# Five moves in the order of DVE and ACT work, and four row transfers as one, in a fused attention and spectral-mix kernel

## The chip, the cores and the metric

One NeuronCore of a Trainium2 chip. The metric is the device time of one execution in microseconds (us), lower is better; where several runs are given, it is their median. The engines are named as the profile names them: PE (TensorE, matmuls), PEld (its weight loads), DVE (VectorE), ACT (ScalarE), POOL (GpSimd), SP (SyncE, which here only issues DMAs). SPq and ACTq are the queues from which DMAs are issued.

## The reference

q, k and v are 8 batches x 12 heads x 448 positions x 64, all float32.

```python
def _attn_ref(q, k, v, cap):
    scale = 1.0 / np.sqrt(q.shape[-1])
    scores = scale * np.matmul(q, k.transpose(0, 1, 3, 2))
    scores = cap * np.tanh(scores / cap)
    scores = scores - np.max(scores, axis=-1, keepdims=True)
    attn = np.exp(scores)
    attn = attn / (np.sum(attn, axis=-1, keepdims=True) + 1e-09)
    return np.matmul(attn, v)

def _moe_ref(x, w_theta, w_tok_r, w_tok_i, w_ch):
    theta = x @ w_theta
    zr, zi = x * np.cos(theta), x * np.sin(theta)
    y = np.einsum('ts,bsd->btd', w_tok_r, zr) + np.einsum('ts,bsd->btd', w_tok_i, zi)
    u = x + y
    return u + np.maximum(u @ w_ch, 0.0)
```

x is the attention's output as 8 x 448 x 768 (the 12 heads side by side).

## The kernel before

**Units.** The attention works on pairs of heads: 48 pairs, numbered k, six of them to a batch, and what a pair gives is one tile X[b, j] of 128 x 448. The mix works on a batch b of six such tiles (j from 0 to 5). A matmul of the mix is made from three products of a high and a low part (`split_x` makes them of X: the high part is a copy on ACT, the low part a subtraction on DVE), and a weight is brought into the same form in steps: a scaling, a `head` of four DVE instructions (L126 to L129), a copy (L131 or L133) and a `rest` of two subtractions (L137, L138).

**Slots.** The program is a row of slots. In slot s the scores of pair s are computed in two halves (on PE; L247, L258 or L268), each with a tanh (ACT, L287) and an exp (ACT, L299 or L293). Both halves use the same accumulator tile `s`, so the next half of scores can start only when the tanh has read the half before. In the same slot the products with v (`av`) and the row sums (`sums`, tile `r`) of pair k = s - 1 run on PE. Slots 0 to 7 are written out in `opening` (L603); from slot 8 on, six slots make a batch, and each takes a line of words from `part_scripts` (L558), one list for batch 0 (slots 8 to 13) and one for batches 1 to 6. What follows the last pair is in `TAIL`. Within the program every engine and every DMA queue runs its instructions in the order in which these words and calls stand (`manual_schedule`): an instruction that waits holds up all that is behind it on its engine.

**The words used below.** SA and SB: the two halves of scores, SB without its tanh, which is tB (with SAm, tA is the tanh of the first half). th, ch: the mix's two projections (`proj`, 18 matmuls a tile). high, low: the two parts of a rotated tile (ACT copy, then DVE subtraction). mix: the product with the token weights (21 matmuls). gain: the residual sum on DVE that reads mix's accumulator and adds it into X (L543). rotate: a DVE multiplication; turn: a transposition on DVE and a DMA to a DRAM buffer; back: four DMAs from it. prep: the split of a q/k pair into two parts on DVE (L216, L217). wa to we: the steps of the weights that stand in `WEIGHTS` for that slot. a, b, c: sums of the exps on DVE. norm: the multiplication of two X tiles by the inverse row sums (L453).

**Accumulators.** `th`, `ch`, `mx`, the sums `r` and the products of odd pairs come from one pool of three buffers (`psM`, L54). A new one takes the buffer of the one three before it, and its first matmul waits for the last reader of that buffer. For a mix, that is a `gain`; for a `ch` tile it is L551 (relu, sum with X, on DVE), which for the last tile of a batch stands behind the six `split_x` of the next batch (L547 to L552).

**Row sums of the first pairs.** For k below 8 a ones-matmul leaves the sums in four rows of an accumulator (0, 32, 64, 96). `invert` (L411) copies it to `rows` (DVE, L419) and four DMAs on SP (L421) reshape each row of 448 to 14 rows of 32 of a small tile. `spread` (L441) takes the reciprocal of that tile on DVE (L438), writes it to DRAM (L433) and reads it back four times as broadcasts (L449, tile `bc`). `norm` (L451) multiplies by `bc`.

**Slots 6 and 7 before** end so (L639 to L651): slot 6 splits X tiles 0 and 1, calls spread(5), then norm(2) and norm(3), then a weight step (a scaling on ACT), then splits tiles 2 and 3. Slot 7 calls norm(4), norm(5) and splits tiles 4 and 5.

Of the kernel before, what the change touches and what calls it, by code (L numbers as in the profile page):

```python
# [36 lines left out]
def softcap_attn_then_spectral_mix(ctx, tc, qk2, v, vj, cap, w_theta, w_tok, w_ch, sel, outT):  # L37
    nc = tc.nc
    B, NP, P, _, S = qk2.shape
# [4 lines left out]
    NJ = DM // P  # L44
# [3 lines left out]
    TB = S // 32  # L48
# [39 lines left out]
    def fill(n):  # L88

        t = psM.tile([P, 512], F32, tag="m", name=f"fill{len(fills)}")  # L90
        fills.append(t)
        for _ in range(n):
            nc.tensor.matmul(t[:32, :CP], ones_sb, ones_sb[:, :1].broadcast_to([CP, CP]), start=True, stop=True)
# [8 lines left out]
    class Split:  # L102
# [37 lines left out]
        def split(self):  # L140
            self.head()
            self.rest()
# [46 lines left out]
    def weights(s, pos):  # L189
        for word in WEIGHTS.get((s, pos), "").split():  # L190
            step = steps[word[-3:-1], int(word[-1])]
            {">": step.load, "*": step.scale, "#": step.vscale, "(": step.head, ")": step.rest}.get(word[0], step.split)()
# [30 lines left out]
    def load_v(k, queue=nc.scalar):  # L223
        if joint(k):
            n = NC3 + k % 2
            vt[k] = wk.tile([P, NC3 + 1, 2, D], F32, tag="v", name=f"v{k}", bufs=2)
            queue.dma_start(vt[k][:, :n], vj[k // NP, k % NP][:, :n])
        else:
            vt[k] = wk.tile([CP, 2, NCH, D], F32, tag="v", name=f"v{k}", bufs=2)
            queue.dma_start(vt[k], v[k // NP, k % NP])  # L230
# [45 lines left out]
    def qk_half(k, half):  # L276

        if not joint(k):
            if (k, half) != (0, 0):
                scores(k, half)  # L280
            rows = slice(0, CP)
        else:
            (quads if k < WHOLE else triples)(k, half)
            rows = slice(0, P)
        pp = pt[k, half] = wk.tile([P, 2, 2, S], F32, tag="xhl" if apart(k, half) else "p", name=f"p{k}_{half}", bufs=3)
        n = 1 if half and joint(k) and not ends(k) else 2
        return lambda: nc.scalar.activation(pp[rows, :n], sp[rows, :n, :, :S], AF.Tanh, scale=qscale[rows])  # L287
# [85 lines left out]
    def copy_x(k):  # L373
        if joint(k) and k % 2 == 0:
            return
        for n in (k - 1, k) if joint(k) else (k,):
            x = wk.tile([P, S], F32, tag="x", name=f"x{n}", bufs=12)
            nc.scalar.copy(x, ACC.pop(n)[:, :S])
            X[n // NP, n % NP] = x
# [3 lines left out]
    def direct(k):  # L383
        return k < DIRECT and not state["general"]
# [26 lines left out]
    def invert(k):  # L411

        if k % 2 == 0:
            return
        r = state.pop("r")
        ri = wk.tile([4 * TB, 32], F32, tag="rq", name=f"rq{k}", bufs=1)
        if direct(k):
            rows = wk.tile([P, S], F32, tag="ri", name=f"ri{k}", bufs=1)
            nc.vector.tensor_copy(rows, r[:, :S])  # L419
            for i in range(4):  # L420
                nc.sync.dma_start(ri[TB * i : TB * (i + 1), :], rows[32 * i : 32 * i + 1, :].rearrange("o (t i) -> o t i", i=32))  # L421
            summed[k] = ri
            return
        if state["general"]:
            nc.vector.tensor_scalar_add(ri, r[: 4 * TB, :32], 1e-9)
            nc.vector.reciprocal(ri, ri)
        else:
            nc.vector.reciprocal(ri, r[: 4 * TB, :32])
        keep(k, ri)

    def keep(k, ri):
        inverse[k] = dram.tile([2, 2, S], F32, tag="inverse", name=f"inverse{k}")
        nc.sync.dma_start(inverse[k].rearrange("n h (t i) -> (n h t) i", i=32), ri)  # L433

    def inverted(k):
        if k in summed:
            ri = summed.pop(k)
            nc.vector.reciprocal(ri, ri)  # L438
            keep(k, ri)

    def spread(k):  # L441
        inverted(k)
        if k not in inverse:
            return
        rows = inverse.pop(k)
        for n in (k - 1, k):
            bc[n] = wk.tile([P, S], F32, tag="bc", name=f"bc{n}", bufs=2)
            for hh in range(2):
                nc.sync.dma_start(bc[n][hh * D : (hh + 1) * D, :], rows[n % 2, hh : hh + 1, :].broadcast_to([D, S]))  # L449

    def norm(k):  # L451
        x = X[k // NP, k % NP]
        nc.vector.tensor_tensor(x, bc.pop(k), x, op=ALU.mult)  # L453
# [4 lines left out]
    def split_x(b, j, name):  # L458
        if j % 2 == 0:
            tag = "p" if name == "xs" and b == B - 1 else "xhl"  # L460
            state["xhl"] = wk.tile([P, 2, 2, S], F32R, tag=tag, name=f"{name}{b}_{j}", bufs=3)
        t = state["xhl"][:, j % 2]
        nc.scalar.copy(t[:, 0, :], X[b, j])
        nc.vector.tensor_tensor(t[:, 1, :], X[b, j], t[:, 0, :].bitcast(F32), op=ALU.subtract)
        XHL[b, j] = t
# [92 lines left out]
    def part_scripts(b):  # L558
        rows = [
# [9 lines left out]
        ]  # L569
        if b == 0:  # L570
            rows = [
# [9 lines left out]
            ]  # L581
        return [row.split() for row in rows]

# [19 lines left out]
    def opening(s):  # L603
        k = s - 1
        qk_half(s, 0)()
        if s == 0:
            fill(FILL["half"])
        weights(s, "a")
        exp_half(s, 0)
        if k >= 0:  # L610
            av(k)
            copy_x(k)
        load_v(s + 1, nc.sync)
        if k >= 0 and not split(k):
            sums(k, (0,))
        qk_half(s, 1)()
        if s == 0:
            fill(FILL["slot"])
        if k >= 0:
            if split(k):  # L620
                sums(k, (0,))
            elif split(k - 1):
                sums(k - 1, (1,))
            else:
                sums(k, (1,))
        load_qk(s + 2)
        weights(s, "b")
        for n in {4: (1,), 6: (3,)}.get(s, ()):
            spread(n)
        if s == 6:  # L630
            weights(s, "c")
        if k >= 0 and not split(k):
            invert(k - 1 if split(k - 1) else k)
            if not direct(k):
                spread(k)
        exp_half(s, 1)
        add_half(s, 0)
        add_half(s, 1)
        if s != 6:  # L639
            weights(s, "c")  # L640
        for n in {5: (0, 1), 7: (4, 5)}.get(s, ()):
            norm(n)
        if s == 6:
            for j in range(2):
                split_x(0, j, "xs")
            spread(5)
            norm(2)
            norm(3)
            weights(s, "d")
        for j in {6: range(2, 4), 7: range(4, NJ)}.get(s, ()):  # L650
            split_x(0, j, "xs")  # L651

    def slot(s):
        k = s - 1
# [138 lines left out]
```

## Time and profile before

| | |
|---|---|
| median of 3 runs | 904.56 us (902.23 to 904.97) |
| the profiled execution | 902.97 us, of which its span in the profile is 901.2 us |
| PE busy | 881.9 us, 98% |
| PEld busy | 656.0 us, 73% |
| DVE busy | 659.1 us, 73% |
| ACT busy | 595.0 us, 66% |
| mean granted TensorE clock | 0.998 |
| HBM, mean over the span | 124 GB/s |

A row of a timeline reads: start (us from the span's start), length in us, engine, line of the kernel, operation, out<-in, shape, count of merged instructions, and in square brackets how long the engine sat idle before it and whose end released it. Rows of one kind that follow each other are merged into one, as x8. Lengths of matmuls are modelled and overlap a little with the next.

### The profile page before, as it was taken

How to read it: one execution, taken by the hardware profiler on the slowest of the kernel's cores; microseconds unless marked ns; L12 is line 12 of the kernel's file. 1: busy time of each engine (PE TensorE's matmuls, PEld its weight loads, DVE VectorE, ACT ScalarE, POOL GpSimd, SP SyncE). 2: the span in 40 equal slices, each digit the busy share in tenths (PEclk: the TensorE clock that was granted, in tenths of full speed). 3: DMA queues.
4: the chain of work that ended last, by engine and by line, in shares of the span. 5: the costliest groups of instructions: out<-in, count | busy, mean ns of one | idle time of the engine just before them, and what ended most of it. 6: DMA issues, size and time to landing. Idle time of an engine off the chain costs nothing.

```text
span 901.2 us, 12590 instructions
## 1 busy us (share of the span) xinstructions
PE 881.9 (98%) x4848; PEld 656.0 (73%) x4848; DVE 659.1 (73%) x940; ACT 595.0 (66%) x599; POOL 1.1 (0%) x7
## 2 busy tenths in 40 slices
PE   8998999999999999999999999999999999999997
PEld 5332767678778777787777787877877877789996
DVE  6886898987975687757977569755897568765841
ACT  6986786578856687647974579546876669744320
POOL 0000000000000000000000000000000000000000
PEclk9999999999999999999999999999999999999999
DMA  7563176323633246132562126522262324501621
GB/s 269 192 199 101 57 260 222 110 88 99 203 91 107 90 132 194 44 122 64 164 193 74 61 72 196 152 85 93 94 205 79 113 84 143 162 19 36 213 64 64
DMA packets 68068, 112.88 MB, mean 125 GB/s; under 512 B 10400, under 2 KB 49824, under 8 KB 68000
## 3 DMA queue, kind: packets, MB, share of 16 engines
q1 hardware_dynamic: 62384, 103.01, 35.8%
q10 hardware_dynamic: 5616, 8.98, 3.3%
q8 instruction: 40, 0.66, 0.3%
q14 instruction: 28, 0.23, 0.1%
HBM read 78.73 MB, written 33.20 MB: 124 GB/s over the span
## 4 chain that ended last, share of the span: by engine, by line
PE 68%; DVE 17%; ACT 6%; DMA 4%; issue 3%; SPq 2%; DVEq 0%; POOL 0%; ACTq 0%; POOLq 0%
PE s L258 8%; PE a L359 6%; PE ch L472 6%; PE ch L474 6%; PE ch L473 6%; PE mx L537 6%; PE mx L538 5%; PE mx L539 5%; PE th L472 4%; PE th L473 4%; PE th L474 4%; DVE g_sb L500 4%; DVE g_sb L507 3%; ACT p L287 3%; PE s L247 3%
## 5 line engine op out<-in xcount | busy, mean ns | idle before, releaser
L287 ACT ACTIVATE p<-s,qscale 128x1792 f32<-128x1792 f32 (+1 forms) x96 | 166.4, 1734 | 119.1 <-PE s L258 106.4
L537 PE MATMUL mx<-wtk_h,zh 128*128 128x448 f32 x336 | 125.5, 374 | 4.2 <-DVE x L543 4.2
L539 PE MATMUL mx<-wtk_h,zl 128*128 128x448 f32 x336 | 123.0, 366 | 0.0
L538 PE MATMUL mx<-wtk_l,zh 128*128 128x448 f32 x336 | 122.8, 366 | 0.0
L472 PE MATMUL ch<-us,wch_h 128*128 128x448 f32 x288 | 107.0, 371 | 0.0
L472 PE MATMUL th<-xs,wth_h 128*128 128x448 f32 x288 | 106.7, 371 | 0.0
L474 PE MATMUL ch<-us,wch_l 128*128 128x448 f32 x288 | 105.7, 367 | 0.9 <-DVE wch_l L138 0.9
L473 PE MATMUL ch<-us,wch_h 128*128 128x448 f32 x288 | 105.7, 367 | 0.0
L474 PE MATMUL th<-xs,wth_l 128*128 128x448 f32 x288 | 105.3, 366 | 0.0
L473 PE MATMUL th<-xs,wth_h 128*128 128x448 f32 x288 | 105.3, 365 | 0.0
L299 ACT ACTIVATE p<-p,cap_sb 128x1792 f32<-128x1792 f32 (+1 forms) x56 | 99.9, 1784 | 0.5
L359 PE MATMUL a<-p,v 128*64 128x448 f32 x480 | 99.0, 548 | 0.0
L537 PEld LDWEIGHTS mx<-wtk_h,zh 128*128 128x128 f32 x336 | 63.1, 188 | 16.5 <-issue 10.7
L529 DVE TENSOR_TENSOR zl<-g_sb,zh 128x896 fp32r<-128x896 f32 x48 | 51.2, 1078 | 32.5 <-ACT zh L523 18.3
L551 DVE SCALAR_TENSOR_TENSOR x<-ch,x 128x448 f32<-128x448 f32 x48 | 29.8, 621 | 59.5 <-PE ch L474 59.5
L359 PEld LDWEIGHTS a<-p,v 128*64 128x64 f32 x480 | 30.9, 136 | 51.5 <-issue 40.9
L539 PEld LDWEIGHTS mx<-wtk_h,zl 128*128 128x128 f32 x336 | 63.1, 188 | 5.3
L538 PEld LDWEIGHTS mx<-wtk_l,zh 128*128 128x128 f32 x336 | 63.1, 188 | 4.9
L523 ACT CAST zh<-g_sb 128x896 fp32r<-128x896 f32 x48 | 44.7, 937 | 26.8 <-PE mx L538 15.9
L472 PEld LDWEIGHTS th<-xs,wth_h 128*128 128x128 f32 x288 | 54.1, 188 | 9.3 <-issue 4.4
L472 PEld LDWEIGHTS ch<-us,wch_h 128*128 128x128 f32 x288 | 54.0, 188 | 9.3 <-issue 3.1
L474 PEld LDWEIGHTS ch<-us,wch_l 128*128 128x128 f32 x288 | 54.1, 188 | 6.2 <-DVE wch_l L138 1.3
(97 smaller groups left out, 1478.7 us busy)
## 6 DMA issues: line engine op xcount, KB each, us to landing
turn<-g_sb SPq DMA_DIRECT2D x48, 448.0 KB
g_sb<-turn SPq DMA_DIRECT2D x192, 112.0 KB
qk_sb<-in_qk SPq DMA_DIRECT2D x39, 448.0 KB
bc<-inverse SPq DMA_DIRECT2D x96, 112.0 KB
out_dram<-x SPq DMA_DIRECT2D x48, 224.0 KB
v<-in_vj ACTq DMA_DIRECT2D x20, 256.0 KB
g_sb<-in_wth SPq DMA_DIRECT2D x6, 768.0 KB
qk<-in_qk SPq DMA_DIRECT2D x9, 448.0 KB
```

What stands on the lines that cost most here:

```text
L258: nc.tensor.matmul(sp[:, i, hh, :S], kk[k][rows, 1, at : at + P], qq[k][rows, 0, :], start=n == 0, stop=n == 2)
L287: return lambda: nc.scalar.activation(pp[rows, :n], sp[rows, :n, :, :S], AF.Tanh, scale=qscale[rows])
L299: nc.scalar.activation(pp[rows], pp[rows], AF.Exp, scale=cap_sb[rows])
L359: nc.tensor.matmul(acc[hh * D : (hh + 1) * D, :S], va[:, c, hh, :], pt[k, c // 2][:, c % 2, hh, :], start=c == 0, stop=False)
L472: nc.tensor.matmul(acc[:, :S], wh[:, j, ms], t[:, 0, :], start=j == 0, stop=False)
L473: nc.tensor.matmul(acc[:, :S], wh[:, j, ms], t[:, 1, :], start=False, stop=False)
L474: nc.tensor.matmul(acc[:, :S], wl[:, j, ms], t[:, 0, :], start=False, stop=j == NJ - 1)
L523: nc.scalar.copy(zh.rearrange("p c (g t) -> p c g t", g=4), turned(j))
L529: nc.vector.tensor_tensor(zl.rearrange("p c (g t) -> p c g t", g=4), turned(j), zh.bitcast(F32).rearrange("p c (g t) -> p c g t", g=4), op ...
L537: nc.tensor.matmul(acc[:, :S], zh[:, c, :], wtk_h[:, c, :], start=c == 0, stop=False)
L538: nc.tensor.matmul(acc[:, :S], zh[:, c, :], wtk_l[:, c, :], start=False, stop=False)
L539: nc.tensor.matmul(acc[:, :S], zl[:, c, :], wtk_h[:, c, :], start=False, stop=c == NC2 - 1)
```

## The change

Five edits of the order, and one of a transfer:

- `invert`: the four DMAs of one row each become one DMA, which reads every 32nd partition of `rows`.
- Slot 6 of `opening`: spread(5) moves behind norm(2) and norm(3). The splits of tiles 2 and 3 move from the end of slot 6 to slot 7, ahead of norm(4) and norm(5).
- Third slot of batches 1 to 6: gain0 moves from behind `turn4 back3` to right behind low2, ahead of rotate4.
- Third slot of batch 0 (slot 10): tA moves ahead of high1.
- Last slot of batch 0 (slot 13): norm moves from ahead of SB, and prep from ahead of `wb`, to behind `wc`.

```diff
-            for i in range(4):
-                nc.sync.dma_start(ri[TB * i : TB * (i + 1), :], rows[32 * i : 32 * i + 1, :].rearrange("o (t i) -> o t i", i=32))
+            nc.sync.dma_start(ri, rows[::32, :].rearrange("n (t i) -> n t i", i=32))
...
-            "SA high0 low0 high1 sincos1 low1 c- V x v SB mix0 high2 tB prep q rotate3 turn3 low2 rotate4 turn4 back3 gain0 r inv"
+            "SA high0 low0 high1 sincos1 low1 c- V x v SB mix0 high2 tB prep q rotate3 turn3 low2 gain0 rotate4 turn4 back3 r inv"
             " rotate5 turn5 back4 back5 bc A B mix1 gain1 mix2",
...
-                "wa SAm fold5 high0 a- low0 high1 tA sincos1 low1 b- V x v SB mix0 c- high2 tB q rotate3 turn3 low2 gain0"
+                "wa SAm fold5 high0 a- low0 tA high1 sincos1 low1 b- V x v SB mix0 c- high2 tB q rotate3 turn3 low2 gain0"
...
-                "SA V x v norm SB tB wa prep q wb A ch3 wc a B ch4 b c ch5",
+                "SA V x v SB tB wa wb A ch3 wc prep q norm a B ch4 b c ch5",
...
-        for n in {5: (0, 1), 7: (4, 5)}.get(s, ()):
-            norm(n)
+        if s == 5:
+            norm(0)
+            norm(1)
         if s == 6:
             for j in range(2):
                 split_x(0, j, "xs")
-            spread(5)
             norm(2)
             norm(3)
+            spread(5)
             weights(s, "d")
-        for j in {6: range(2, 4), 7: range(4, NJ)}.get(s, ()):
-            split_x(0, j, "xs")
+        if s == 7:
+            for j in range(2, NJ):
+                if j == 4:
+                    norm(4)
+                    norm(5)
+                split_x(0, j, "xs")
```

## Rows read from the trace of the kernel before

**Rows 1.** Page, busy us (share) xinstructions; PE's waits: total us, times, longest.

```profile
PE 881.9 (98%) x4848; PEld 656.0 (73%) x4848; DVE 659.1 (73%) x940; ACT 595.0 (66%) x599; POOL 1.1 (0%) x7
...
PE mx L537 <- DVE x L543: 4.2, 6, 0.7
```

**Rows 2.** Timeline of PE, slots 2 and 6 to 8.

```profile
21.94 1.76 PE L247 MATMUL s<-qk_sb 64*112 64x448 f32 x8 [1.85 <-ACT p L287]
...
70.82 1.70 PE L404 MATMUL r<-p,ones_sb 112*32 112x448 f32 x8
76.70 2.60 PE L247 MATMUL s<-qk 64*112 64x448 f32 x8 [4.18 <-ACT p L287]
...
81.66 1.74 PE L268 MATMUL s<-qk_sb 64*64 64x448 f32 x16
...
89.61 0.98 PE L268 MATMUL s<-qk_sb 64*64 64x448 f32 x8
```

**Rows 3.** Timeline of ACT in slots 6 to 8.

```profile
73.90 1.09 ACT L463 CAST xs<-x 128x448 fp32r<-128x448 f32 x2 [4.71 <-DVE x L453]
74.90 1.75 ACT L287 ACTIVATE p<-s,qscale 112x1792 f32<-112x1792 f32 x1
...
79.46 1.74 ACT L287 ACTIVATE p<-s,qscale 112x1792 f32<-112x1792 f32 x1
...
86.42 1.75 ACT L287 ACTIVATE p<-s,qscale 128x1792 f32<-128x1792 f32 x1
```

**Rows 4.** Timeline of DVE in slots 6 and 7.

```profile
68.23 1.16 DVE L464 TENSOR_TENSOR xs<-x,xs 128x448 fp32r<-128x448 f32 x2 [1.75 <-ACT xs L463]
73.04 0.34 DVE L438 RECIPROCAL rq<-rq 56x32 f32<-56x32 f32 x1 [3.65 <-DMA rq<-ri]
...
75.57 0.39 DVE L126 TENSOR_SCALAR swk_t<-swk_raw 128x448 int32<-128x448 int32 x1
...
84.76 1.15 DVE L453 TENSOR_TENSOR x<-bc,x 128x448 f32<-128x448 f32 x2
```

**Rows 5.** Timeline of SP's DMA queue in slot 6.

```profile
68.57 3.25 SPq L421 DMA_DIRECT2D rq<-ri  x4
```

**Rows 6.** Windows: us, busy PE, PEld, DVE, ACT, POOL, PEclk (granted clock), DMA share, GB/s.

```profile
77.50:80.90 3.40, 3.40 (x12) 0.87 (x10) 3.26 (x7) 3.40 (x3) 0.00 (x0) 0.50 0.79 256
```

**Rows 7.** Timelines of ACT and PE in slot 10.

```profile
121.79 0.94 ACT L523 CAST zh<-g_sb 128x896 fp32r<-128x896 f32 x1 [1.17 <-DMA g_sb<-turn]
...
124.44 0.98 PE L268 MATMUL s<-qk 64*64 64x448 f32 x8 [0.86 <-ACT p L287]
```

**Rows 8.** Timelines of DVE, ACT and PE in slots 13 and 14.

```profile
181.07 1.15 DVE L453 TENSOR_TENSOR x<-bc,x 128x448 f32<-128x448 f32 x2
...
183.88 0.55 DVE L126 TENSOR_SCALAR g_sb<-g_sb 128x768 int32<-128x768 int32 x1
...
197.76 0.62 DVE L551 SCALAR_TENSOR_TENSOR x<-ch,x 128x448 f32<-128x448 f32 x1
...
182.30 0.91 ACT L118 ACTIVATE g_sb<-g_sb 128x768 f32<-128x768 f32 x1
...
189.46 0.47 PE L474 MATMUL ch<-us,wch_l 128*128 128x448 f32 x1 [0.93 <-DVE wch_l L138]
...
199.29 0.47 PE L472 MATMUL th<-xs,wth_h 128*128 128x448 f32 x1
```

**Rows 9.** Timelines of DVE and PE in slots 16 and 17 (batch 1).

```profile
240.01 1.08 DVE L500 TENSOR_TENSOR g_sb<-g_sb,x 128x896 f32<-128x896 f32 x1
...
242.16 0.59 DVE L543 TENSOR_TENSOR x<-mx,x 128x448 f32<-128x448 f32 x1
...
259.98 1.08 DVE L529 TENSOR_TENSOR zl<-g_sb,zh 128x896 fp32r<-128x896 f32 x1
...
242.90 0.44 PE L537 MATMUL mx<-wtk_h,zh 128*128 128x448 f32 x1 [0.70 <-DVE x L543]
...
261.65 0.37 PE L539 MATMUL mx<-wtk_h,zl 128*128 128x448 f32 x1
```

## The prediction, made before the changed kernel was run

> **What bounds the kernel now.** I read the page first, then PE's waits, then the timelines around each wait. PE is busy 98% of the span [rows 1], in nearly every slot, and its instructions are not changed. So the time is PE's work plus the places where PE stands still, and each edit is worth what it takes from such a place, less what it opens at another. The list of waits is short. Six times PE waits up to 0.70 us for a residual sum, 4.2 us in all [rows 1], once in the third slot of each of batches 1 to 6. Once it waits 4.18 us for a tanh in slot 7 [rows 2], once 0.86 us for a tanh in slot 10 [rows 7], once 0.93 us for a weight's low part in slot 13 [rows 8]. The reader is to see in these rows the bracket (how long, released by whom) and then, on the releaser's engine, what stood ahead of the releaser. DVE and ACT are at 73% and 66% [rows 1]: they have room on average, and cost only by order.
>
> **The opening (slots 6 to 8).** The tanh that PE waits for ran at 74.90, but ACT was idle from 73.90 - 4.71 = 69.19 [rows 3]: two copies of X tiles stood ahead of it, which need norm(2) and norm(3), and these stood behind a reciprocal on DVE that sat idle 3.65 us until 73.04 for the four row DMAs [rows 4]. These had been issued from 68.57 on and took 3.25 us to issue [rows 5].
> After the change the two copies are in slot 7, so the tanh runs from 69.2 to 70.95, and PE goes on right behind the sums of 70.82, at 72.5 instead of 76.70: the 4.18 us are gone. Those eight score matmuls took 2.60 us behind the gap, against 1.76 behind a gap of 1.85 us [rows 2], and from 77.5 to 80.9 the granted clock was 0.50, the 1.2 GHz level [rows 6]: it fell in the long gap. From 76.70 to 81.66 it took 4.96 us for what takes about 1.7 + 1.65 at full speed; that 1.6 us goes too. The second tanh of slot 7 is 4.56 us behind the first on ACT [rows 3], so ready to run at 73.8, before its scores end at 74.2. It ends at 76.0, and the first scores of slot 8 start at 76.05 instead of 81.66. The next scores are 7.95 us behind them [rows 2]: 84.0.
> There a new wait opens. Their tanh stands on ACT behind the copies of tiles 4 and 5, and these behind norm(4), norm(5). On DVE: the subtractions for tiles 0 and 1 end at 69.4 [rows 4]; norm(2), norm(3) take 1.1 (as at 84.76) and end at 70.5 (their broadcasts stand ahead of 68.57 on SP's queue [rows 5]). The reciprocal follows. Its DMA: one of the four takes 3.25 / 4 = 0.81 to issue, and the reciprocal came 1.2 us behind the last issue (71.82 to 73.04) [rows 4, 5], so 68.57 + 0.81 + 1.2 = 70.6, and the reciprocal ends at 70.95. The splits of two weights take 84.76 - 75.57 = 9.19 [rows 4], until 80.1; the subtractions of tiles 2 and 3 take 1.16, until 81.3; then norm(4), norm(5). Before, the tanh followed the start of these by 86.42 - 84.76 = 1.66 [rows 3, 4]: 83.0, and ends at 84.7. So the scores of 89.61 start at 84.7, 0.7 us late: **gain 4.9 us**. norm(4) stands 10.3 us behind the reciprocal of its sums, against 11.7 before, with the write and the broadcasts between; I take that as covered.
> The cost of one DMA of four rows is in no row. Above: it takes as long to issue as the four, the reciprocal stays at 73.04, all behind it is 2.1 us later, and the gain is 2.8. Below: it is free, but then norm(3) ends last at 70.5, and DVE gains only 0.1; if no wait at all were left, 5.6. I take 0.81, the row of the same reshaping. For the other pairs (1, 3, 7) the reciprocal is not followed back to PE, and I cost the DMAs saved on SP at nothing: PE's matmuls beside them cover it.
> The Trainium skill's page "DMA: Bandwidth & Descriptors" (section "Why a DMA increments its semaphore by 16 and not by 1") speaks against this part: such a DMA runs on the largest number of the 16 engines that divides the outermost dimension of both sides. With four rows outermost that is at most four engines, 14 pieces each; no row here shows on how many engines a reshaping ran. By that rule the transfer lands later than 70.6, towards the 2.8 end; by the rows it is 4.9.
>
> **Slot 10.** ACT sat idle 1.17 us until 121.79, for a DMA in front of high1 [rows 7], with the tanh behind it. In front of it the tanh runs from 120.62 to 122.4 (1.75, [rows 3]), and PE wants it at 124.44 - 0.86 = 123.58: **gain 0.86**. high1 is 0.6 us later; it is for the second mix tile, and the 21 matmuls of the first cover it. Without that cover it would cost 0.6.
>
> **Slot 13.** The `head` of the last weight started on DVE at 183.88, behind norm and prep, which began at 181.07: 2.81 us. Its scaling on ACT ended at 182.30 + 0.91 = 183.21 [rows 8]. With norm and prep behind `wc`, the head starts at 183.25, only 0.63 earlier, and so does the matmul of 189.46; 0.3 of the wait stays. The 2.81 us do not vanish: they now stand ahead of the rest of the slot on DVE, where before, from 183.88 to 197.76, no row shows it idle. So the L551 that reads the last `ch` tile ends not at 197.76 + 0.62 = 198.38 but at 198.38 - 0.63 + 2.81 = 200.56. Three accumulators further on, its buffer is that of the first `th` tile of batch 1 (ch5, products of pair 13, sums of pair 13, th0). PE reaches this tile at 199.29 - 0.63 = 198.66 [rows 8], where 0.9 us were left before; it starts at about 200.7 (0.15 from the end of a DVE instruction to PE's start, as 242.75 to 242.90 [rows 9]). A new wait of 2.05, against 0.63 won: **loss 1.4 us**. The six low parts of `th0` stand ahead of L551 on DVE and are done by then. After 1.85 us of idle time the clock was still full, after 4.18 not [rows 2]; the cost of that here is 0 to 1.6, and I take 0, as 2.05 is nearer the first.
>
> **The third slots of batches 1 to 6.** The third mix tile takes the buffer of the first, so it waits for gain0: it ran at 242.16, behind rotate4 and turn4, which began at 240.01, and PE started at 242.90 after 0.70 [rows 9]. Right behind low2 it runs from 240.01 to 240.6, before PE wants it at 242.20: 0.70 x 6 = 4.2. What is late next: rotate4 and turn4 are 0.53 us later (240.01 to 240.6 less a small overlap), with turn4's DMA, and behind it on SP back3, the inverse sums, turn5, back4 and back5. Along back4, the low part of tile 4 and that of tile 5 (DVE, until 259.98 + 1.08 = 261.06), this reaches the first matmul of mix5 that reads a low part, at 261.65: 0.59 us of room [rows 9]. If that chain hangs wholly on the DMAs, it is at 261.59 when PE comes at 260.95, and 0.64 of the 0.70 goes back; if it hangs on PE, nothing does. The row is that of batch 1 alone. I take 0.8 us given back in all six, between 0 and 4.2, as the row's chain starts from both: **gain 3.4 us**.
>
> **Sum.** 4.9 + 0.86 - 1.4 + 3.4 = 7.8 us. Against the profiled execution (902.97, a span of 901.2 and 1.8 around it): 895.2. The three runs (902.23, 904.56, 904.97) and this one have a mean of 903.7, and from there it is 895.9, which I predict for a median. A measurement of this kernel can tell about 0.3%, 2.7 us, from no change.
>
> **The rivals.**
> - **th0 is not held.** For: another buffer could be free, or L551 sooner. Against: the waits of 0.70 fit three buffers in turn. Then slot 13 gains 0.63 instead of losing 1.4: 893.9.
> - **The one DMA is slow** (2.1 us later reciprocal, by the bound above). For: no row shows such a DMA, and 56 pieces on few engines take longer than on many. Against: one DMA of a row took 0.81 us to issue and about 1.2 to land, and this one moves only four of these rows. 898.0. The rule of the Trainium skill's page "DMA: Bandwidth & Descriptors" (same section) would make it this one.
> - **The batches give all back** before mix5, in place of the wait removed. For: 0.59 us of room against 1.2 us by which the two sides move. Against: most of that chain starts from PE. 899.3.
> - **Nothing measurable:** the two last together, with a lost clock at th0: 895.9 + 2.1 + 3.4 + 1.6 = 903.0.
> - **Slower.** One mechanism: turn4's later DMA lets the four DMAs of back4 fall behind another transfer in every batch, and mix5 waits. A DMA ahead of a high part held ACT 1.17 us in slot 10 [rows 7]. The other terms give 4.9 + 0.86 - 1.4 + 4.2 = 8.6, so it decides from 1.43 us per batch; at 2.2 us it is 13.2 - 8.6 = +4.6, 908.3. Against: the chain's own delay is 0.64.
>
> **How the numbers follow.** Forecast 0.50, th0 free 0.14, slow DMA 0.12, batches give back 0.10, nothing 0.09, slower 0.05. Faster by over 0.3% (under 901.8) are the first four: 0.86; within 0.09; slower 0.05. The range leaves out the last two and little of the others: from 891.5 (th0 free, no wait in the opening, nothing given back: 893.9 - 0.7 - 0.8, and a little below) to 900.5 (all given back, and half of the 2.7 us above).
>
> **What would show it.** Right: no wait before the second scores of slot 7 and none with a fallen clock; a wait of 0.3 to 1 us before the second scores of slot 8; none in slot 10; about 0.3 us at the last weight's matmul in slot 13, and about 2 us before th0 of batch 1, released by DVE L551; no wait for L543 in six batches, and in some a wait of up to 0.6 before mix5. Wrong: the reciprocal of pair 5 after 72, a th0 that starts without a wait, or new waits of over 1 us inside the batches.

## The result, and the profile after

The changed kernel takes 890.17 us in the median of four runs (889.06 to 891.45), beside 904.76 us (902.23 to 904.99) for the kernel before: ratio 0.9846, 95% interval 0.9823 to 0.9868. Predicted were 895.9 us and a range from 891.5 to 900.5: the sign was right, the gain about twice the forecast, and the time 1.3 us below the range. The profiled execution took 889.06 us, with a span of 887.3 us. Line numbers behind L420 are one lower than before the change.

The page (busy us, share, instructions) and PE's waits (us in total, times, longest):

```profile
PE 876.6 (99%) x4848; PEld 656.2 (74%) x4848; DVE 658.1 (74%) x940; ACT 594.2 (67%) x599; POOL 1.1 (0%) x7
...
PE s L247 <- ACT p L287: 3.2, 7, 1.9
PE s L268 <- ACT p L287: 1.2, 2, 0.9
PE fill L93 <- POOL ones_sb L98: 0.9, 1, 0.9
PE ch L473 <- DVE wch_l L138: 0.3, 1, 0.3
```

The line for the residual sums [rows 1] is gone, and no line has taken its place. The same 4848 matmuls have 5.3 us less busy time. Part of that is the half clock of the opening, which is gone, and part belongs to the pauses: the matmul ahead of a pause counts as busy up to its modelled end. The rest is a change in the pace of the matmuls.

The opening, in timelines of PE, DVE, ACT and SP's queue (start, length, engine, line, operation, operands, count, and in brackets the idle time ahead and who ended it), to hold against [rows 2 to 5]:

```profile
70.84 1.70 PE L404 MATMUL r<-p,ones_sb 112*32 112x448 f32 x8
72.47 1.76 PE L247 MATMUL s<-qk 64*112 64x448 f32 x8
...
76.09 1.73 PE L268 MATMUL s<-qk_sb 64*64 64x448 f32 x16 [0.23 <-ACT p L287]
...
85.06 0.98 PE L268 MATMUL s<-qk_sb 64*64 64x448 f32 x8 [0.95 <-ACT p L287]
...
70.52 0.63 DVE L452 TENSOR_TENSOR x<-bc,x 128x448 f32<-128x448 f32 x1 [0.51 <-DMA bc<-inverse]
71.06 0.34 DVE L437 RECIPROCAL rq<-rq 56x32 f32<-56x32 f32 x1
...
81.60 1.15 DVE L452 TENSOR_TENSOR x<-bc,x 128x448 f32<-128x448 f32 x2
...
82.25 1.10 ACT L462 CAST xs<-x 128x448 fp32r<-128x448 f32 x2 [2.95 <-DVE x L452]
...
83.26 1.75 ACT L287 ACTIVATE p<-s,qscale 128x1792 f32<-128x1792 f32 x1
...
68.25 0.59 SPq L420 DMA_DIRECT2D rq<-ri  x1
```

The scores at 72.47 stand directly behind the sums, and take 1.76 us, the time at full clock. The one DMA took 0.59 us to issue; the reciprocal waited for it not at all. The chain forecast for the new wait is there, link by link: norm, copies, tanh, scores.

Slot 10 (ACT, PE) and slots 13 and 14 (PE, DVE), to hold against [rows 7, 8]:

```profile
116.19 1.75 ACT L287 ACTIVATE p<-s,qscale 128x1792 f32<-128x1792 f32 x1
...
119.07 0.93 PE L268 MATMUL s<-qk 64*64 64x448 f32 x8
...
183.38 0.47 PE L473 MATMUL ch<-us,wch_l 128*128 128x448 f32 x1 [0.28 <-DVE wch_l L138]
...
193.21 0.47 PE L471 MATMUL th<-xs,wth_h 128*128 128x448 f32 x1
...
194.42 0.62 DVE L550 SCALAR_TENSOR_TENSOR x<-ch,x 128x448 f32<-128x448 f32 x1
```

The last two rows are where the prediction broke: th0 of batch 1 starts at 193.21 without a wait, 1.2 us before the residual sum that should have held it has even begun.

Where the 13.9 us between the two profiled executions lie: subtract the start of each matmul after from that of the same matmul before, and see where the difference moves.

| up to | difference, us | step | forecast |
|---|---|---|---|
| the second scores of slot 8 | 4.56 | +4.56 | +4.9 |
| the th tiles of slot 9 (206.7 ns a matmul after, 202.7 before) | 4.34 | -0.22 | 0 |
| slot 10, second scores and the first step behind them | 5.43 | +1.09 | +0.86 |
| slot 13, the last weight | 6.08 | +0.65 | +0.63 |
| th0 of batch 1 | 6.08 | 0 | -2.05 |
| six third slots (batches 1 to 6) | 12.20 | +6.12 | +3.4 |
| the end, from ch0 of the last full batch on | 13.96 | +1.76 | 0 |

### The profile page after: what moved, and what is told of

It is laid out like the page before. It is cut to its first block, busy times and chain, and to the rows that moved or that the text cites. A ratio compares the mean times of both kernels' runs of the same rounds, so it can differ in the third digit from the quotient of the medians.

```text
span 887.3 us, 12578 instructions
## 1 busy us (share of the span) xinstructions
PE 876.6 (99%) x4848; PEld 656.2 (74%) x4848; DVE 658.1 (74%) x940; ACT 594.2 (67%) x599; POOL 1.1 (0%) x7
## 4 chain that ended last, share of the span: by engine, by line
PE 93%; ACT 2%; DVE 2%; issue 1%; DMA 1%; SPq 0%; ACTq 0%; POOL 0%; DVEq 0%; POOLq 0%
PE s L258 11%; PE a L359 11%; PE mx L536 8%; PE mx L538 8%; PE mx L537 8%; PE th L471 7%; PE th L473 7%; PE th L472 7%; PE ch L471 7%; PE ch L473 6%; PE ch L472 6%; PE a L365 2%; PE s L247 2%; PE s L268 2%; ACT p L287 2%; PE a L370 1%
## 5 line engine op out<-in xcount | busy, mean ns | idle before, releaser
L550 DVE SCALAR_TENSOR_TENSOR x<-ch,x 128x448 f32<-128x448 f32 x48 | 29.8, 620 | 58.7 <-PE ch L473 58.7
```

## The experiments

**The first residual sum alone.** The kernel before, with gain0 moved in batches 1 to 6 and nothing else.

```diff
-... rotate3 turn3 low2 rotate4 turn4 back3 gain0 r inv"
+... rotate3 turn3 low2 gain0 rotate4 turn4 back3 r inv"
```

> The kernel before with gain0 alone moved ahead of rotate4 in batches 1 to 6. Theory A (a wait inside a row of matmuls costs more than its bracket): the bracket of 0.70 counts from the modelled end of a matmul (0.365 us long), but matmuls of this stretch start every 0.203 us, so each wait costs 0.70 + 0.365 - 0.203 = 0.86, and the 21 matmuls behind it ran at 0.2067 instead of 0.2027, another 0.08 to 0.15. Six of them: 5.2 to 6.1 us less, no wait for L543, and no wait of PE before the low part of mix5. Theory B (that of the prediction): 4.2 us less at PE's wait, and up to 0.64 us a batch given back before mix5, so 3.4 less, with waits at L539.

Measured: 896.04 us (894.94 to 897.23) beside 903.67, ratio 0.9913 [0.9896, 0.9930], so 7.6 us. PE's waits:

```profile
PE s L247 <- ACT p L287: 7.4, 8, 4.2
...
PE mx L539 <- DVE zl L529: 0.2, 1, 0.2
```

Almost nothing is given back: of the late chain to mix5 one wait of 0.2 us shows in the whole program, in batch 4, where the starts lose 0.44 us; the six places themselves give 5.9 us by the starts. The opening's wait stands as before. The 7.6 us are more than the six waits can give (6.1 by the next experiment). In the profiled execution (896.60 us) this kernel's end ran at the faster pace, of which below; at which pace it ran in the other three is not shown.

**The first residual sum put back**, in batches 1 to 6 of the changed kernel: the same two lines the other way round.

> The changed kernel with the first residual sum of batches 1 to 7 back behind the last transfers of its slot, as before the change. Theory (a wait for L543 costs more than its bracket says): six waits of 0.69 to 0.92 us come back ahead of the third part of six batches, each costs 0.86 us by the starts of the matmuls around it and 0.15 us more by the slower pace of the 21 matmuls behind it, so +6.1 us, about 896.3 us, ratio 0.991. Rival (the prediction's account, 0.57 a batch, with part of it given back in the same slot): +3.4 us, 893.6 us, ratio 0.988.

Measured: 894.93 us (894.40 to 895.48), ratio 0.9916 [0.9894, 0.9939]: 4.8 us over the changed kernel by the medians, 6.3 by the ratios. Start for start against the trace of the changed kernel, the stretch of the six places costs 6.08 us, some 1.0 each, and the rest is a 0.68 us shorter opening in this execution. Timeline of PE at the first place with gain0 behind, and in the changed kernel (last row):

```profile
235.06 0.37 PE L538 MATMUL mx<-wtk_h,zl 128*128 128x448 f32 x1
236.14 0.44 PE L536 MATMUL mx<-wtk_h,zh 128*128 128x448 f32 x1 [0.71 <-DVE x L542]
236.42 0.37 PE L537 MATMUL mx<-wtk_l,zh 128*128 128x448 f32 x1
```
```profile
235.94 0.36 PE L536 MATMUL mx<-wtk_h,zh 128*128 128x448 f32 x1
```

The bracket says 0.71, but the starts stand 1.08 apart where 0.20 is usual: 0.87 us are lost. The idle time is counted from the modelled end of a matmul, 0.36 us behind its start, while the next one starts 0.20 behind. The rest of the 1.0 us lies behind the wait. The first step there is 0.28 us (236.14 to 236.42) instead of 0.20, and at this and two more of the six places the matmuls that follow in the tile run at 206.7 ns in place of 202.7, which is another 0.08 us; at the other three they run at 202.7. So a place costs 0.94 to 1.03 us.

**The opening alone** (the one DMA, spread(5) behind two norms, the splits in slot 7), in the kernel before.

> The kernel before with the edits of slots 6 and 7 and the single row DMA alone. If the opening's account holds by itself: the wait of 4.18 us and the fallen clock behind it are gone (5.6 us at the first scores of slot 8), a wait of 0.7 to 1.0 us stands before the second scores of slot 8, and 4.4 to 4.9 us are left at the end. The waits of slots 10 and 13 (0.86, 0.93) and the six of 0.70 stay. Rival: the moves give more because later waits shrink with them; then more than 5.5 us.

Measured: 898.35 us (896.50 to 900.26), ratio 0.9933 [0.9917, 0.9950], 5.3 us beside a forecast of 4.9; start for start against the trace of the kernel before, this opening is 4.67 us shorter. PE's waits keep the six for the residual sum and lose the long one:

```profile
PE mx L536 <- DVE x L542: 4.4, 6, 0.9
PE s L247 <- ACT p L287: 3.2, 7, 1.9
```

**The four DMAs put back**, in the changed kernel.

```diff
-            nc.sync.dma_start(ri, rows[::32, :].rearrange("n (t i) -> n t i", i=32))
+            for i in range(4):
+                nc.sync.dma_start(ri[TB * i : TB * (i + 1), :], rows[32 * i : 32 * i + 1, :].rearrange("o (t i) -> o t i", i=32))
```

> The changed kernel with its four row DMAs back in place of the one. Theory (the one DMA shortens the way to the reciprocal of pair 5): in the changed kernel SP issued the rows in 0.59 us from 68.25 and the reciprocal began at 71.06 without a wait; four issues took 3.25 us in the kernel before and the reciprocal began 1.2 us behind the last of them, so it would begin at about 72.7, 1.65 us later, and carry all of DVE behind it, the copies at 82.25 and the tanh of slot 8: the wait ahead of its second scores grows from 0.95 to about 2.6 us and the kernel takes about 891.8 us, ratio to the kernel before 0.986 to 0.987. Rival (one DMA over four rows lands as late as four): the reciprocal at 71.1 and no change, 890.2 us, ratio 0.9846.

Measured: 893.40 us (892.09 to 895.78), ratio 0.9906 [0.9880, 0.9932]. DVE, PE and SP's queue:

```profile
73.67 0.35 DVE L438 RECIPROCAL rq<-rq 56x32 f32<-56x32 f32 x1 [1.85 <-DMA rq<-ri]
...
87.61 0.98 PE L268 MATMUL s<-qk_sb 64*64 64x448 f32 x8 [2.80 <-ACT p L287]
...
69.20 3.25 SPq L421 DMA_DIRECT2D rq<-ri  x4
```

The wait ahead of the second scores is 2.80 us, 1.85 more than with one DMA: just what DVE now waits for the transfers. So the one DMA is worth 1.85 us at this place, and the rival of a slow one falls. The median lies 3.2 us over the changed kernel's (5.4 by the ratios); three of the four executions had a mean granted clock of 0.997 beside 0.999 in the profiled one (892.09 us), so behind this longer gap the clock may have fallen in them, which no trace of them shows. By the Trainium skill's page "DMA: Bandwidth & Descriptors" (section "Why a DMA increments its semaphore by 16 and not by 1") one DMA with four rows outermost runs on at most four engines. No row shows on how many it ran, and DVE never waited for it.

**Slot 13 alone** (norm and prep behind `wc`), in the kernel before.

> The kernel before with norm and prep alone moved in slot 13. Theory C (the buffer of an accumulator is not the one three before it but the one that the build expects to be free first): th0 of batch 1 gets the buffer of pair 13's products, not that of ch5, does not wait for L551, and the edit is worth the 0.65 us by which the last weight's head starts earlier. Rival (that of the prediction, buffers in fixed turn): th0 waits about 2 us for L551, and the kernel is 1.4 us longer.

Measured: 902.66 us (901.26 to 904.91), ratio 0.9996 [0.9984, 1.0007]. The wait ahead of the last weight shrinks as in the changed kernel, 0.28 us, and th0 of batch 1 has none. The loss of 1.4 us is not there. Its reason shows in the built programs, where each accumulator's bank can be read. In the kernel before, th0 of batch 1 does have ch5's bank, as the prediction says. In this kernel and in the changed one it has the bank of the products of pair 13: moving the DVE work of slot 13 has also changed which buffer the build gives to th0. So buffers do not go round in fixed turn, against what it says under "Accumulators"; in the kernel before too, ch0 of batch 0 has the bank of the products of pair 11, two before it. That the build takes the buffer it expects to be free first would fit all of this; the rule itself is not shown.

**Buffers in fixed turn**, in the changed kernel: one buffer for each of three tags, handed out in turn.

```diff
+    turns = itertools.count()
+    def acc_tile(name):
+        return psM.tile([P, 512], F32, tag=f"m{next(turns) % 3}", name=name, bufs=1)
...
-        acc = psM.tile([P, 512], F32, tag="m", name=f"{name}{b}_{m}")
+        acc = acc_tile(f"{name}{b}_{m}")
```

> The changed kernel with the three accumulator buffers handed out strictly in turn (three names, one buffer each), all else as it is. Theory C: th0 of batch 1 then takes ch5's buffer and starts 0.1 to 0.2 us behind the end of L551, a wait of about 2 us on PE, so the span is about 2 us more than 887.3. Rival (th0 could start early for another reason, L551 sooner than thought): no wait there, 887.3 to 888.

Measured: 895.03 us (891.91 to 896.31), ratio 0.9908 [0.9892, 0.9925]. PE and DVE at th0 of batch 1:

```profile
196.00 0.47 PE L476 MATMUL th<-xs,wth_h 128*128 128x448 f32 x1 [1.76 <-DVE x L555]
...
195.32 0.62 DVE L555 SCALAR_TENSOR_TENSOR x<-ch,x 128x448 f32<-128x448 f32 x1
```

The predicted wait is there, from the predicted instruction and near the predicted size (1.83 by the starts, beside 2.05). The median is 4.9 us over the changed kernel's (5.6 by the ratios), more than this wait: a second one, 1.2 us ahead of a ch tile of batch 0, opens with the fixed turn, and the executions behind the profiled one (891.91 us, mean clock 0.998) had 0.996 to 0.997. The account of DVE was right; what failed was the buffer that th0 would get.

**Buffers in fixed turn, in the kernel before**, as a control.

> The kernel before with the accumulators in fixed turn, a new one always in the buffer of the one three before it. Control for the same edit on the changed kernel, which cost 4.9 us, 1.9 of them at th0 of batch 1. Theory (the residual sum of ch5 holds th0 only where the change has moved it late): no wait ahead of th0 of batch 1 here, and the rest of the cost as there, so about +3.0 us, 907 us, ratio 1.003. Rival (the fixed turn costs th0 the same whatever the order on DVE): a wait of 1.8 us ahead of th0 of batch 1 and +4.9 us, 909 us, ratio 1.005.

Measured: 903.71 us (901.70 to 905.17) beside 902.13, ratio 1.0011 [0.9999, 1.0023]. The fixed turn costs 0 to 2 us here, less than both readings said; the second wait, 1.2 us, is here too. th0 of batch 1 has no wait (PE, DVE):

```profile
202.21 0.47 PE L477 MATMUL th<-xs,wth_h 128*128 128x448 f32 x1
...
200.70 0.62 DVE L556 SCALAR_TENSOR_TENSOR x<-ch,x 128x448 f32<-128x448 f32 x1
```

The sum of ch5 is done at 201.32, 0.9 us ahead of PE, the margin that the prediction read. So slot 13's move does push it behind PE; only with a fixed turn does that cost anything.

**The pace of the end.** In both kernels five small matmuls into an unread part of the scores' buffer interrupt the last stream, one ahead of each of ch1 to ch5 of the last batch.

```diff
     def chan(b, m):
+        if b == B - 1 and m > 0:
+            nc.tensor.matmul(sp[:32, 0, 0, S : S + 16], ones_sb, ones_sb[:, :16], start=True, stop=True)
```

> The kernel before with one small matmul (16 columns, into a part of the scores' buffer that nothing reads) ahead of each of ch1 to ch5 of the last batch. In the profiled execution of the kernel before all matmuls from 803 us on stood 206.7 ns apart, where the changed kernel had 202.7 ns, which makes 1.7 us. Theory (the pace is a state of the stream that holds until something interrupts it): the pace of ch1 to ch5 is no longer that of ch0 in all of them, some groups at 202.7 and some at 206.7 ns, and the kernel takes between 0.7 us less and 0.3 us more than before. Rival (the pace belongs to the operands, the program or the execution as a whole): all six groups stand at one pace.

> The changed kernel with the same five small matmuls. In its profiled execution ch0 to ch5 of the last batch stood 202.7 ns apart. Theory (the pace is a state that holds until the stream is interrupted, and may come out either way): some of ch1 to ch5 stand 206.7 ns apart, each such group costing 0.07 us; the time is that of the changed kernel within 0.5 us. Rival (the pace belongs to the operands, the program or the execution as a whole): all six groups at one pace, that of ch0.

Measured: 903.88 us beside 903.32 (ratio 1.0011 [1.0000, 1.0022]), and 890.95 (0.9869 [0.9852, 0.9885]). In both traces the 70 us up to and with ch0 stand 206.7 ns apart, and each of ch1 to ch5, from its second matmul on, 202.7. Windows of the kernel before with the five matmuls, ch0 and then ch1 (us, busy time of PE, PEld, DVE, ACT, POOL; granted clock; DMA share, GB/s):

```profile
874.48:877.99 3.51, 3.51 (x18) 3.19 (x17) 1.25 (x2) 0.57 (x1) 0.00 (x0) 1.00 0.01 2
878.76:882.00 3.24, 3.24 (x17) 3.00 (x16) 0.26 (x1) 0.00 (x0) 0.00 (x0) 1.00 0.22 76
```

From first to last start, 17 steps take 3.51 us (206.5 ns) and 16 steps 3.24 (202.5), both at a granted clock of 1.00. So the pace belongs neither to the operands nor to the execution as a whole, and a small matmul left the stream at the faster one in ten of ten cases. That only an interruption changes it is not shown: in eight of the other 12 traces it changes within the first tile of the last stretch (from ch0 of batch 6 on) with no other matmul in between, and the waits for the residual sum left the slower pace at four of six places in the kernel before and at three of six with gain0 put back. Each small matmul cost some 0.35 us between its neighbours, more than it gave back, so both times lie above what was expected. That the unmarked part of the changed kernel's end is slow in this execution, and was fast in the first, the next pair shows in full.

**A better version, and the changed kernel again beside it.** The copies and low parts of tiles 4 and 5 go behind the tanh of slot 8's first half; the two norms stay.

```diff
-                "SA V x v r inv SB tB q wb bc A th0 fold0 a B th1 fold1 b wc th2",
+                "SA xs V x v r inv SB tB q wb bc A th0 fold0 a B th1 fold1 b wc th2",
...
-            for j in range(2, NJ):
-                if j == 4:
-                    norm(4)
-                    norm(5)
-                split_x(0, j, "xs")
+            for j in range(2, 4):
+                split_x(0, j, "xs")
+            norm(4)
+            norm(5)
...
+            if e == "xs":
+                for j in range(4, NJ):
+                    split_x(b, j, "xs")
```

> The changed kernel with the copies and low parts of tiles 4 and 5 of batch 0 put behind the tanh of slot 8's first half; the two norms ahead of them stay in their place. Theory (the second scores of slot 8 wait 0.95 us because that tanh stands on ACT behind two copies that wait 2.95 us for a norm): the tanh runs from about 79.3, the scores have no wait, the copies still run at about 82.25, ahead of their first reader in th0; the kernel takes 0.95 to 1.1 us less than the changed one, about 889.1 us, ratio to the kernel before 0.983. Rival (something else is late next: the sums copied from r on DVE at 84.18, or the tiles 4 and 5 that th0 reads from about 88.0): the wait moves to th0 and nothing is won, 890.2 us, ratio 0.9846.

> The changed kernel once more, on one chip beside the version with the copies of tiles 4 and 5 behind the tanh. Expected by both readings: 890 us within 1.5 us, ratio to the kernel before 0.983 to 0.987. The last 100 us stand at 206.7 or at 202.7 ns a matmul by chance, which is 1.7 us of difference between executions.

> The version with the copies and low parts of tiles 4 and 5 behind the tanh of slot 8's first half, on the same chip as the changed kernel. Theory (the wait ahead of the second scores of slot 8 was worth its 0.95 us and nothing took its place): a median 0.5 to 1.5 us below the changed kernel's. Rival (the 1.4 us between the two traces lay in the start of the run): no difference beyond 0.3 us; the starts of matmuls in the two traces differ as much ahead of 80 us as behind 90 us.

Measured: 889.18 us (887.71 to 890.38), ratio 0.9855 [0.9832, 0.9878]; then, on one chip, the changed kernel 891.08 (889.95 to 892.07), 0.9866 [0.9845, 0.9887], and this version 889.91 (887.96 to 891.03), 0.9850 [0.9832, 0.9869]. PE and ACT in the first of these runs:

```profile
83.54 0.98 PE L268 MATMUL s<-qk_sb 64*64 64x448 f32 x8
...
78.70 1.75 ACT L287 ACTIVATE p<-s,qscale 128x1792 f32<-128x1792 f32 x1
...
81.18 1.10 ACT L462 CAST xs<-x 128x448 fp32r<-128x448 f32 x2 [0.74 <-DVE x L452]
```

The wait is gone, and the starts move at this place by 1.02 us in the first pair of traces and by 1.19 in the second. So 1.0 to 1.2 us are won there. Elsewhere the pairs differ as much: by 0.50 and 0.92 us in the first 8 us, ahead of the edit, and in the second pair by 1.0 us more at a late transfer in the changed kernel. The medians differ by 1.0 and 1.2, but the intervals of the ratios overlap, and the first ratio lies above the changed kernel's 0.9846: on the whole time the gain is not shown.

The second pair settles the end. First and last matmul of the stretch from ch0 to the end, changed kernel, first execution and the one beside the better version:

```profile
790.70 0.47 PE L471 MATMUL ch<-us,wch_h 128*128 128x448 f32 x1
...
881.83 0.37 PE L473 MATMUL ch<-us,wch_l 128*128 128x448 f32 x1
```
```profile
791.74 0.47 PE L471 MATMUL ch<-us,wch_h 128*128 128x448 f32 x1
...
884.62 0.37 PE L473 MATMUL ch<-us,wch_l 128*128 128x448 f32 x1
```

The same program took 91.13 and 92.89 us for it. So did the better version, and in the 12 traces without the small matmuls no other value occurs: 91.13 eight times, 92.88 four times, the kernel before among the latter. The last 1.76 us of the table are an accident of the two executions.

## Why the prediction was wrong

**The opening: right.** Forecast 4.9, the trace gave 4.56, the run with this part alone 5.3 between medians. The scores of slot 7 came at 72.47 (forecast 72.5), those of slot 8 at 76.09 (76.05), the reciprocal ended at 71.4 (70.95), held 0.51 us by a broadcast that I had put down as done. That carried to the second scores, 85.06 against 84.7. The one DMA was the open price between 4.9 and 2.8; with four in the same order the starts are 1.85 us later, so the value taken was right. Of the 4.56 us, 0.22 went again in slot 9, where the th tiles ran at the slower pace in the trace after the change.

**Slot 10: right,** with 1.09 by the starts for a bracket of 0.86. **Slot 13's first half: right,** 0.65 against 0.63, with 0.28 of the wait left as forecast.

**th0 of batch 1: the step that failed.** "Three accumulators further on, its buffer is that of the first `th` tile" was inferred from six waits that fit three buffers in turn. It holds in the kernel before as built; the step took it to hold after the edit as well, and there the build gave th0 the buffer of pair 13's products. The DVE chain was right (L550 at 194.42 after; the fixed turn gave 1.76 us), the buffer was not, and 2.05 us of loss weren't there. This was the first rival, with a chance of 0.14 and 893.9 us.

**The batches: a term mis-sized, in two ways.** 3.4 us were forecast, 6.12 came. The six brackets of 0.70 cost 0.86 each by the starts, 0.08 at the step behind, and at four of the six places 0.08 of pace: 0.94 to 1.03 instead of 0.70. And 0.8 us were booked as given back ahead of mix5, where no wait came up in the changed kernel's trace. The 0.59 us of room was that of batch 1 alone, the smallest of the six; the others had 0.87 to 2.60. After the change the rooms are 0.12 to 2.59. In batch 4 the room fell by 0.75, as if the chain hung wholly on the DMAs (0.64), and 0.87 just covered it; in batch 1 it grew to 0.85. So how far the chain follows PE differs between batches, and only the room kept PE from waiting. DVE and PE in batch 4, before and after:

```profile
579.96 1.08 DVE L529 TENSOR_TENSOR zl<-g_sb,zh 128x896 fp32r<-128x896 f32 x1
...
581.91 0.37 PE L539 MATMUL mx<-wtk_h,zl 128*128 128x448 f32 x1
```
```profile
570.63 1.08 DVE L528 TENSOR_TENSOR zl<-g_sb,zh 128x896 fp32r<-128x896 f32 x1
...
571.84 0.40 PE L538 MATMUL mx<-wtk_h,zl 128*128 128x448 f32 x1
```

**The end: not foreseen.** 1.76 us of the 13.96 between the last starts are the pace of the last 450 matmuls, which the change doesn't touch. Without them the pair differs by 12.2 us, and 902.97 - 12.2 = 890.8 would still lie below the range. The errors add up: 2.05 (th0) + 2.72 (batches) + 1.76 (end) - 0.34 (opening) - 0.22 (slot 9) + 0.23 (slot 10) + 0.02 (slot 13) = 6.22, which is 13.96 less the 7.74 of the unrounded forecast. The lower end of the range took in a free th0, no wait in the opening and nothing given back (892.4), but no price of a wait beyond its bracket and no difference of pace.

## What to carry to other kernels

On an engine with pipelined work, price a wait by the distance of the starts around it and not by the bracket, and look whether the stream behind it runs at the same pace. Where a wait depends on which buffer a tile gets, read the buffer from the built program, and from that of the changed kernel too, as an edit of the order can change it; a pattern of waits that fits a rule doesn't prove it. A difference of one or two microseconds between two single executions is read start for start first: part of it may lie where the edit can't reach.

## What the runs showed of the hardware

**Two paces.** Streams of matmuls of 128 x 448 with a weight load each run at 202.7 or at 206.7 ns from start to start, at a granted clock of 1.00 both times, and kept their pace for up to 92.9 us. The Trainium skill's page "TensorE: Matmul & The Clock Gate" (section "Back-to-back issue gap") gives N / 2.4 + 2.5 ns for an isolated matmul, an estimate of 189 ns for 448 columns; no stream of these shows it. What chooses the pace was not found: in all 14 traces the last stretch begins at the slower one, behind the small matmul of the row sums, and in eight of them it changes within the first tile, while the added small matmuls left the faster one in ten of ten cases.

**The clock and the length of a gap.** Behind 2.80 us of idle PE the granted clock was 1.00 (the four DMAs put back, in the one execution with a trace), behind 4.18 [rows 2, 6] and 4.22 us 0.50, the 1.2 GHz level; three more traces with such a gap, of 4.28 to 4.68 us, show 0.50 behind it too. Windows of the first kernel with gain0 alone, from the scores behind the 4.22 us, and of the kernel with four DMAs, from those behind the 2.80 us:

```profile
77.00:80.30 3.30, 3.30 (x10) 1.11 (x12) 3.16 (x7) 2.84 (x3) 0.00 (x0) 0.50 0.72 222
```
```profile
87.61:89.50 1.89, 1.89 (x13) 1.12 (x14) 1.79 (x5) 1.18 (x2) 0.00 (x0) 1.00 0.02 3
```

**Single late transfers.** In the second execution of the changed kernel the second mix tile of batch 4 waited 0.94 us for a copy on ACT that stood behind a high part, held 1.94 us by a DMA; in the first execution ACT stood 0.50 us there and PE didn't wait. The trace of the opening alone has the same wait, 0.8 us, at the same tile. So a late high part can hold PE, as the rival "slower" feared, but at another place than mix5, and the move of gain0 isn't needed for it.
